# A retention layer and a gated feed-forward block on one core: the steps of a hand-written order split by engine and put in a new order

## The chip, the cores and the metric

The kernel runs on one core of a Trainium2 chip. A core has five engines that run their own instruction lists and wait for each other through semaphores: PE (matrix products, with weight loads, PEld, beside them), DVE (vector), ACT (scalar functions and copies), POOL (GpSimd, which here also issues the loads), and SP (which issues the stores and the DMA transposes). The metric is the device time of one execution in microseconds. The profile is of one execution.

## The reference

```python
def _attn_ref(q, k, v):                       # 4 x 8 x 768 x 64
    gamma = 1.0 - 2.0 ** (-5.0 - np.arange(H, dtype=np.float32))
    scale = 1.0 / np.sqrt(D)
    ...
    for t in range(S):
        state = gamma[None, :, None, None] * state + np.einsum('bhd,bhe->bhde', k[:, :, t], v[:, :, t])
        y[:, :, t] = scale * np.einsum('bhd,bhde->bhe', q[:, :, t], state)
...
def _moe_ref(x, w_gate, w_val, w_out):        # 3072 x 512, 512 x 1536, 1536 x 512
    gate = 1.0 / (1.0 + np.exp(-(x @ w_gate)))
    val = x @ w_val
    return (gate * val @ w_out).astype(np.float32)
```

The attention's output, with the heads side by side as 512 features of 3072 tokens, is the input x of the feed-forward part. Inputs and outputs are float32.

## The kernel before

**Tiling.** The sequence is cut into 6 chunks of 128 positions. A chunk of all four batches is one stage t: 512 tokens. Its attention is done in two halves, P = 2t and 2t + 1, of two batches each; c is the batch in a half. So P runs from 0 to 11 and t from 0 to 5.

**Attention of a half P.** `load` brings k, q and v to SBUF as bf16 (three DMAs on POOL's queue). The transposes of k and q, `qkT`, come from PE (`transposes`, evicted by ACT) for the first halves and from DMA transposes on SP's queue (`xbar`) for P from 4 on. `scores` (16 matmuls for each c, into two PSUM banks) give q times k; `masks` (DVE, line 208) multiply them by the decay table `maskd` and free the banks; `inter` and `intra` (lines 217, 223) add the part of the carried state and of the chunk itself; `y_out` (DVE, line 238) writes the result into `xT`, the transposed input of the feed-forward part. `scaled` (ACT, line 194, or DVE, line 190) weights k, `state` (PE) multiplies it with v, `state_sum` (DVE) adds to the running state `za`, and `state_out` (ACT, line 260) copies it to `zbd`. `tile_tables` (POOL, lines 151 and 155) builds the decay tables of a stage.

**Feed-forward of a stage t.** There are 12 groups of 128 hidden features. A gate product goes through a sigmoid (ACT) and is multiplied with a value product (DVE or POOL) into `hT`. Stages 0 and 2 and the last two groups of stages 3 to 5 use `up`, whole products; stage 1 works in halves of 256 tokens (`up_half`); stages 3 to 5 make the value products of two groups at a time with seven half-size products (`val_product`, a fast matrix multiplication), which need sums of the weights (`val_weight_sums`, POOL, `ws`) and of x (`x_sums`, DVE, `xs`), with ACT copies and DVE additions between the products (lines 395 to 407). The second matrix product of a stage, `product` with `fast_out`, is done in the same way with seven products for each of two token blocks i; it needs `hidden_sums` (DVE, line 438, `hs`) and `weight_sums` (POOL and ACT, `wt`). For block 1 of stage 0 it is done plainly (`down`), and the hidden sums of stage 0 (`s`) are of 128 columns instead of 256. Between product 5, 6, 7 and 4 of a block lie an ACT copy (lines 480 to 494, tile `p`) and a DVE addition (lines 481 to 490, tile `ob`) that read the bank onto which the next product adds. In stages 1 to 4 `mm` splits each matmul of 128 columns in two of 64.

**Order.** The kernel is scheduled by hand: each engine runs its instructions in the order in which the program issues them. After a fixed beginning (first loads, tables, the attention of P = 0 and 1, the first group of stage 0, and the loads up to P = 5) the strings in ORDER, one for each stage, list steps. A step is a letter and a number; `-` puts it in the stage before, `@` names a stage. A step issues all that belongs to it on all engines: `u3` is a gate product, a value product, the sigmoid and the multiply of group 3; `B5` is the scores, inter, intra, state products, masks, y_out and state sum of a half; `X5` is product 5 of block 0 with its copy and addition. `H` (`hold`) and `I` keep POOL waiting until the DMA transposes of a half, or a stage's hidden sums, are there, before the next loads or weight sums.

**Room.** PSUM has 7 banks for all of this (`bank`, pool `pf`) and one for the states; a product's step begins when one of the seven is free. There are 4 buffers each of k, q, v and qkT, two of kt, six for sigmoids (`gs`), two for `scr`, four for `ob`.

Of the kernel before, what the change touches and what calls it, by code (L numbers as in the profile page):

```python
# [17 lines left out]
def kernel(  # L18
# [10 lines left out]
    nc = tc.nc  # L29
# [118 lines left out]
    def tile_tables(t):  # L148
        maskd[t] = at.tile([128, 2, NP, C], F32, tag="maskd", name="maskd")
        for i in range(2):  # L150
            nc.gpsimd.affine_select(maskd[t][:, i], tabk[:, t, i:H:2].unsqueeze(2).to_broadcast([128, NP, C]),
                                    pattern=[[0, NP], [1, C]], base=0, channel_multiplier=-1,
                                    compare_op=ALU.is_ge, fill=0.0)
        taby[t] = at.tile([128, NP, C], F32, tag="taby", name="taby")
        nc.gpsimd.tensor_tensor(taby[t], taby0, tabz[:, t, :].unsqueeze(2).to_broadcast([128, NP, C]), op=ALU.mult)
# [11 lines left out]
    def transposes(P, i, cs, *evict):  # L167
        tp = bank([128, 2 * NP, C], BF16).rearrange("d (c p) s -> d c p s", c=2)
        x = (kn, qn)[i][P].rearrange("s g d -> s (g d)")
        for c in cs:  # L170
            for p in range(NP):
                nc.tensor.transpose(tp[:, c, p, :], x[:, (c * NP + p) * C:(c * NP + p + 1) * C], ident)  # L172
        if len(evict) == 1:
            cs = [slice(cs[0], cs[-1] + 1)]
# [3 lines left out]
    def xbar(P):  # L178
        new_qkT(P)
        for i, x in enumerate((kn, qn)):  # L180
            nc.sync.dma_start_transpose(out=qkT[P][:, i].rearrange("d c p s -> d (c p) s"),
                                        in_=x[P].rearrange("s g d -> s (g d)"))

    def scaled(P, part, eng=None):
        x = kn[P].rearrange("s (c h) d -> s c h d", c=2)
        if part in (None, 0):
            kt[P] = ld.tile([C, 2 * H, D], BF16, tag="kt", name="kt", bufs=2)
        to = kt[P].rearrange("s (c h) d -> s c h d", c=2)
        if part is None:
            eng.tensor_tensor(to, x, tabk[:, P // 2, :].unsqueeze(1).unsqueeze(3).to_broadcast([C, 2, H, D]),  # L190
                              op=ALU.mult)
            return
        for h in range(part * NP, (part + 1) * NP):
# [9 lines left out]

    def masks(P, c):
        st[P, c] = []
        for i in range(2):
            s = at.tile([128, NP, C], BF16, tag="st", name="st", bufs=8)
            nc.vector.tensor_tensor(s, sc[P, c][i], (mask0 if P < 2 else maskd[P // 2])[:, i], op=ALU.mult)  # L208
            st[P, c].append(s)
# [10 lines left out]
    def intra(P, c):  # L220
        for p in range(NP):
            for i in range(2):
                nc.tensor.matmul(y[P, c][i * D:(i + 1) * D, p, :], heads(vn[P], c)[:, 2 * p + i, :],  # L223
                                 st[P, c][i][:, p, :], start=(P < 2 and p == 0), stop=True, skip_group_check=True)
# [31 lines left out]
    def state_out(P):  # L256
        j = P % 2
        for i in range(2):
            half = slice(i * D, (i + 1) * D)
            nc.scalar.copy(zbd[j][half, :, :, half], za[j][half])  # L260

    def has_state(P):
        return P is not None and P < NPAIR - 2

    def block(done, new, sum_now=True):
        if new is not None:
            for c in range(2):
                scores(new, c)
        if done is not None:
            for c in range(2):  # L270
                inter(done, c)
            for c in range(2):
                intra(done, c)
        if has_state(new):
            state(new)
        if new is not None:
            for c in range(2):
                masks(new, c)
        if done is not None:
            for c in range(2):  # L280
                y_out(done, c)
        if has_state(new) and sum_now:
            state_sum(new)
# [15 lines left out]
    def up(t, n1, lo=0, hi=512, finish=True):  # L299
        if t not in hT:  # L300
            hT[t] = ffn.tile([128, NFF, 512], BF16, tag="hT", name="hT", bufs=2)
        ps = []
        for w in (wg, wv):
            u = bank([128, 512])
            for kk in range(KT):
                mm(t, u[:, lo:hi], w[:, kk, n1 * 128:(n1 + 1) * 128], xT[t][:, kk, lo:hi],
                   start=(kk == 0), stop=(kk == KT - 1))
            ps.append(u)
        gs = ffn.tile([128, 512], F32, tag="gs", name="gs", bufs=6)
        gated[t, n1] = (hT[t][:, n1, lo:hi], gs[:, lo:hi], ps[1][:, lo:hi], ps[0][:, lo:hi])  # L310
        if finish != "none":
            up_sigmoid(t, n1)
        if finish is True:
            up_finish(t, n1)

    def up_sigmoid(t, n1):
        nc.scalar.activation(gated[t, n1][1], gated[t, n1][3], AX.Sigmoid)  # L317

    def up_finish(t, n1):
        to, gs, val, _ = gated.pop((t, n1))  # L320
        nc.vector.tensor_tensor(to, gs, val, op=ALU.mult)  # L321

    def up_half(t, n1, half):
        lo = half * 256
        if t not in hT:
            hT[t] = ffn.tile([128, NFF, 512], BF16, tag="hT", name="hT", bufs=2)
        ps = []
        for w in (wg, wv):
            u = bank([128, 2, 256])
            for i in range(2):  # L330
                for kk in range(KT):
                    mm(t, u[:, i], w[:, kk, (n1 + i) * 128:(n1 + i + 1) * 128], xT[t][:, kk, lo:lo + 256],
                       start=(kk == 0), stop=(kk == KT - 1))
            ps.append(u)
        gs = ffn.tile([128, 2, 256], F32, tag="gs", name="gs", bufs=6)
        nc.scalar.activation(gs, ps[0], AX.Sigmoid)
        nc.vector.tensor_tensor(hT[t][:, n1:n1 + 2, lo:lo + 256], gs, ps[1], op=ALU.mult)
# [3 lines left out]
    def val_weight_sums(g, eng):  # L341
        lo, hi = (slice(n * 128, (n + 1) * 128) for n in (2 * g, 2 * g + 1))
        a11, a12, a21, a22 = wv[:, :2, lo], wv[:, 2:, lo], wv[:, :2, hi], wv[:, 2:, hi]
        s1, s2, s3, s4 = (ws[:, g, i] for i in range(4))
        eng.tensor_tensor(s1, a21, a22, op=ALU.add)
        eng.tensor_tensor(s2, s1, a11, op=ALU.subtract)
        eng.tensor_tensor(s3, a11, a21, op=ALU.subtract)
        eng.tensor_tensor(s4, a12, s2, op=ALU.subtract)
# [3 lines left out]
    def x_sums(t):  # L352
        xs[t] = ffn.tile([128, 4, KT // 2, 256], BF16, tag="xs", name="xs", bufs=1)
        b11, b12, b21, b22 = (xT[t][:, kk:kk + 2, c:c + 256] for kk in (0, 2) for c in (0, 256))
        t1, t2, t3, t4 = (xs[t][:, i] for i in range(4))
        nc.vector.tensor_tensor(t1, b12, b11, op=ALU.subtract)
        nc.vector.tensor_tensor(t3, b22, b12, op=ALU.subtract)
        nc.vector.tensor_tensor(t2, b22, t1, op=ALU.subtract)
        nc.vector.tensor_tensor(t4, b21, t2, op=ALU.subtract)

    sig, vals = {}, {}

    def gate(t, n1):
        if t not in hT:
            hT[t] = ffn.tile([128, NFF, 512], BF16, tag="hT", name="hT", bufs=2)
        u = bank([128, 512])
        for kk in range(KT):
            mm(t, u, wg[:, kk, n1 * 128:(n1 + 1) * 128], xT[t][:, kk, :], start=(kk == 0), stop=(kk == KT - 1))
        sig[n1] = ffn.tile([128, 512], F32, tag="gs", name="gs", bufs=6)
        nc.scalar.activation(sig[n1], u, AX.Sigmoid)  # L370

    def val_product(t, g, n):
        lo, hi = (slice(i * 128, (i + 1) * 128) for i in (2 * g, 2 * g + 1))
        if n == 1:
# [301 lines left out]
```

## Time and profile before

| What | Value |
|---|---|
| median of 3 runs | 222.43 us (221.85 to 222.57) |
| profiled execution, first to last instruction | 221.5 us |
| PE busy | 209.5 us, 95% |
| PEld busy | 161.7 us, 73% |
| DVE busy | 158.4 us, 72% |
| POOL busy | 123.7 us, 56% |
| ACT busy | 116.8 us, 53% |
| second half of the first feed-forward group begins on PE | 17.65 us |
| software DMA queue (loads), share of 16 engines | 82.4% |
| hardware DMA queue (stores and transposes) | 27.5% |
| granted TensorE clock | 1.00 |

Busy shares are of the span of 221.5 us. A wait in the lists is the idle time of an engine ahead of an instruction, with what ended it. In the chain each row has a start, a length and what ran. DMA shares of the two queues are of the time that packets took and may add to more than one.

### The profile page before, as it was taken

The numbers are of one execution on the slowest core, as the hardware profiler recorded it, in microseconds if no ns is written. First come the engines' busy times: TensorE is split into PE (matmuls) and PEld (weight loads), VectorE is DVE, ScalarE is ACT, GpSimd is POOL, SyncE is SP. The second block draws the span as 40 slices with busy tenths as digits, with TensorE's granted clock in tenths as the row PEclk, the third lists the DMA queues.
The fourth block names the chain that finished last, engine by engine and source line by source line (L and its number), as shares of the span: only waits on it lengthen the run. The fifth ranks groups of instructions, "written<-read, shape, count | busy, mean of one in ns | idle before, by whom it ended". The sixth has DMA issues, their size and how long they took to land.

```text
span 221.5 us, 6886 instructions
## 1 busy us (share of the span) xinstructions
PE 209.5 (95%) x2924; PEld 161.7 (73%) x2924; DVE 158.4 (72%) x326; ACT 116.8 (53%) x250; POOL 123.7 (56%) x141
## 2 busy tenths in 40 slices
PE   6558999999998999999999999999999999999993
PEld 6444445799997777767779877789877777866682
DVE  6764876988659596465997579898577797544861
ACT  7584375437794336445397277635345525465231
POOL 8966886769997606999400896540243331325500
PEclk9999999999999999999999999999999999999999
DMA  9999999999995999719999899930310000220014
GB/s 126 134 172 194 196 173 156 195 186 157 132 119 53 139 198 140 215 47 120 126 134 199 136 186 157 124 73 0 145 52 0 3 3 0 95 98 0 1 44 150
DMA packets 103999, 25.35 MB, mean 114 GB/s; under 512 B 93984, under 2 KB 101152, under 8 KB 103968
## 3 DMA queue, kind: packets, MB, share of 16 engines
q0 software_dynamic: 81248, 13.90, 82.4%
q1 hardware_dynamic: 22576, 10.88, 27.5%
q8 instruction: 23, 0.38, 0.7%
q10 hardware_dynamic: 144, 0.13, 0.2%
q14 instruction: 8, 0.07, 0.2%
HBM read 28.31 MB, written 6.29 MB: 156 GB/s over the span
## 4 chain that ended last, share of the span: by engine, by line
PE 86%; DVE 5%; DMA 4%; POOL 3%; issue 0%; ACT 0%; POOLq 0%; DVEq 0%
PE ff L297 52%; PE ff L293 25%; DMA vn<-in_v_dram 4%; PE ff L201 2%; PE ff L217 2%; PE ff L223 2%; DVE xT L238 2%; PE z L245 1%; DVE hs L438 1%; DVE st L208 1%; POOL vn L64 1%; POOL kn L64 1%; POOL qn L64 1%; POOL kn L72 0%; PE ff L172 0%
## 5 line engine op out<-in xcount | busy, mean ns | idle before, releaser
L297 PE MATMUL ff<-xT,wg 128*64 128x512 bf16 (+1 forms) x480 | 50.3, 337 | 0.3 <-DVE xT L238 0.2
L401 POOL TENSOR_TENSOR hT<-gs,scr 128x512 bf16<-128x512 f32 x15 | 19.4, 1293 | 35.4 <-DVE scr L400 35.4
L297 PE MATMUL ff<-xT,wv 128*64 128x256 bf16 (+1 forms) x400 | 35.6, 307 | 1.0 <-DVE st L208 1.0
L297 PEld LDWEIGHTS <-wg 128*64 128x64 bf16 x480 | 27.7, 110 | 7.3 <-issue 0.3
L297 PEld LDWEIGHTS <-wv 128*64 128x64 bf16 x440 | 26.2, 110 | 8.8 <-issue 1.2
L321 DVE TENSOR_TENSOR hT<-gs,ff 128x512 bf16<-128x512 f32 (+1 forms) x31 | 20.6, 666 | 15.0 <-ACT gs L317 6.0
L370 ACT ACTIVATE gs<-ff 128x512 f32<-128x512 f32 x30 | 17.9, 597 | 22.3 <-PE ff L297 12.9
L317 ACT ACTIVATE gs<-ff 128x512 f32<-128x512 f32 (+1 forms) x31 | 17.8, 582 | 20.6 <-PE ff L297 11.5
L293 PE MATMUL ff<-xT,wg 128*128 128x512 bf16 (+1 forms) x100 | 25.0, 371 | 1.5 <-ACT xT L236 0.9
L208 DVE TENSOR_TENSOR st<-ff,maskd 128x512 bf16<-128x512 f32 x40 | 24.8, 682 | 1.5 <-PE ff L201 1.5
L297 PEld LDWEIGHTS <-hT 128*64 128x64 bf16 x384 | 21.4, 110 | 3.8
L405 POOL TENSOR_TENSOR hT<-gs,scr 128x256 bf16<-128x256 f32 x15 | 11.3, 756 | 12.5 <-DVE scr L404 12.5
L293 PE MATMUL ff<-xT,wv 128*128 128x512 bf16 (+1 forms) x80 | 17.5, 342 | 0.0
L260 ACT CAST zbd<-za 64x512 bf16<-64x512 f32 x20 | 12.3, 616 | 8.8 <-DVE za L252 3.2
L297 PE MATMUL ff<-wo,hT 128*64 128x256 bf16 (+1 forms) x216 | 16.2, 296 | 0.0
L293 PEld LDWEIGHTS <-wg 128*128 128x128 bf16 x100 | 9.4, 98 | 9.2 <-issue 0.9
L64 POOL DMA_DIRECT2D vn<-in_v_dram x12 | 14.0, 1170 | 2.9 <-PE ff L297 1.7
L194 ACT ACTIVATE kt<-kn,tabk 128x128 bf16<-128x128 bf16 x48 | 15.2, 390 | 0.1
L64 POOL DMA_DIRECT2D kn<-in_k_dram x11 | 12.9, 1173 | 3.2 <-DMA vn<-in_v_dram 1.5
L297 PEld LDWEIGHTS <-hs 128*64 128x64 bf16 x252 | 14.0, 110 | 0.9
L293 PEld LDWEIGHTS <-wv 128*128 128x128 bf16 x90 | 8.8, 98 | 7.6 <-issue 0.2
L64 POOL DMA_DIRECT2D qn<-in_q_dram x11 | 12.7, 1158 | 1.3 <-issue 0.6
(108 smaller groups left out, 412.3 us busy)
## 6 DMA issues: line engine op xcount, KB each, us to landing
out_dram<-ob SPq DMA_DIRECT2D x22, 256.0 KB, 2.6
vn<-in_v_dram POOLq DMA_DIRECT2D x12, 256.0 KB, 12.1
kn<-in_k_dram POOLq DMA_DIRECT2D x11, 256.0 KB, 8.5
qn<-in_q_dram POOLq DMA_DIRECT2D x11, 256.0 KB, 11.8
wo<-in_moe_w_out_dram POOLq DMA_DIRECT2D x4, 384.0 KB, 13.0
wg<-in_moe_w_gate_dram POOLq DMA_DIRECT2D x5, 256.0 KB, 9.8
wv<-in_moe_w_val_dram POOLq DMA_DIRECT2D x5, 256.0 KB, 9.5
out_dram<-ob SPq DMA_DIRECT2D x3, 128.0 KB, 2.2
```

Source lines behind the costliest of these rows:

```text
L64: nc.gpsimd.dma_start(out=held[P], in_=src(x, P))
L194: nc.scalar.activation(to[:, :, h, :], x[:, :, h, :], AX.Copy, scale=tabk[:, P // 2, h:h + 1])
L201: nc.tensor.matmul(sc[P, c][i][:, p, :], qkT[P][half, 0, c, p, :], qkT[P][half, 1, c, p, :], start=True, stop=True)
L208: nc.vector.tensor_tensor(s, sc[P, c][i], (mask0 if P < 2 else maskd[P // 2])[:, i], op=ALU.mult)
L260: nc.scalar.copy(zbd[j][half, :, :, half], za[j][half])
L293: nc.tensor.matmul(o, left, right, skip_group_check=True, **kw)
L297: nc.tensor.matmul(o[half], left[:, half], right, skip_group_check=True, **kw)
L317: nc.scalar.activation(gated[t, n1][1], gated[t, n1][3], AX.Sigmoid)
L321: nc.vector.tensor_tensor(to, gs, val, op=ALU.mult)
L370: nc.scalar.activation(sig[n1], u, AX.Sigmoid)
L401: nc.gpsimd.tensor_tensor(hT[t][:, 2 * g], sig[2 * g], v[:, 0:2].rearrange("p two n -> p (two n)"), op=ALU.mult)
L405: nc.gpsimd.tensor_tensor(hT[t][:, 2 * g + 1, 256:], sig[2 * g + 1][:, 256:], v[:, 2], op=ALU.mult)
```

## The change

Each function that issued work on several engines is split, so that a step issues one operation, or the matmuls of one product. A step's name has two letters now, and `+` and `-` after its number move it a stage later or earlier (twice for two). The 1016 steps of ORDER are all written in a new order. The fixed beginning has the same instructions in the same order. No instruction is added or removed; the compiled lists have the same numbers of each operation on each engine, with 2924 matmuls, and the same DMAs on each queue (54 on POOL's, 43 on SP's, one on ACT's). The core of the diff:

```diff
-    def tile_tables(t):
-        maskd[t] = at.tile([128, 2, NP, C], F32, tag="maskd", name="maskd")
-        for i in range(2):
+    def tile_tables(t, i):
+        if i < 2:
+            if t not in maskd:
+                maskd[t] = at.tile([128, 2, NP, C], F32, tag="maskd", name="maskd")
...
+    def mask(P, c, i):
+        st[P, c, i] = at.tile([128, NP, C], BF16, tag="st", name="st", bufs=8)
+        nc.vector.tensor_tensor(st[P, c, i], sc[P, c][i], (mask0 if P < 2 else maskd[P // 2])[:, i], op=ALU.mult)
...
-    def up(t, n1, lo=0, hi=512, finish=True):
...
+    def up(t, n1, which, lo=0, hi=512):
+        if (t, n1, which) not in us:
+            us[t, n1, which] = bank([128, 512])
+        w = (wg, wv)[which]
+        for kk in range(KT):
+            mm(t, us[t, n1, which][:, lo:hi], w[:, kk, n1 * 128:(n1 + 1) * 128], xT[t][:, kk, lo:hi],
+               start=(kk == 0), stop=(kk == KT - 1))
...
-    def hidden_sums(t, g, n=256, parts=range(4)):
+    def hidden_sums(t, g, i, n=256, eng=nc.vector):
...
-        for i in parts:
-            o, x, z, op = ops[i]
-            nc.vector.tensor_tensor(o, x, z, op=op)
+        eng.tensor_tensor(o, x, z, op=op)
...
-    def fast_out(t, i, n):
+    def fast_copy(t, i, n):
...
+    def fast_add(t, i, n):
...
+    def fast_store(t, i, n):
...
     STEPS = {
-        "u": lambda t, n: up(t, n),
-        "a": lambda t, n: up_half(t, n, 0),
-        "S": lambda t, g: hidden_sums(t, g),
-        "s": lambda t, g: hidden_sums(t, g, 128),
-        "X": lambda t, n: products(t, (0, n)),
-        "B": lambda t, P: block(P - 1, P if P < NPAIR else None),
...
+        "gm": lambda t, n: up(t, n, 0),
+        "vm": lambda t, n: up(t, n, 1),
+        "sg": lambda t, n: up_sigmoid(t, n),
+        "mu": lambda t, n: up_finish(t, n),
+        "ag": lambda t, n: up_half(t, n, 0, 0),
+        "av": lambda t, n: up_half(t, n, 0, 1),
+        "as": lambda t, n: half_sigmoid(t, n, 0),
+        "am": lambda t, n: half_finish(t, n, 0),
...
+        "vp": lambda t, n: half_product(t, n // 10, n % 10, 1),
+        "vc": lambda t, n: val_copy(t, n // 10, n % 10),
+        "va": lambda t, n: val_add(t, n // 10, n % 10),
+        "vf": lambda t, n: val_finish(t, n // 10, n % 10),
+        "aw": lambda t, n: halves_sums(wv, n // 4, ws[:, n // 4], n % 4),
+        "xs": lambda t, n: x_sums(t, n),
+        "hs": lambda t, n: hidden_sums(t, n // 4, n % 4),
+        "hh": lambda t, n: hidden_sums(t, n // 4, n % 4, 128),
+        "wp": lambda t, n: weight_sums(n // 4, n % 4),
+        "dp": lambda t, n: product(t, n // 10, n % 10),
+        "dc": lambda t, n: fast_copy(t, n // 10, n % 10),
+        "da": lambda t, n: fast_add(t, n // 10, n % 10),
+        "ds": lambda t, n: fast_store(t, n // 10, n % 10),
+        "dm": lambda t, n: down(t, n // 2, n % 2),
...
+        "lk": lambda t, P: load(P, "k"),
+        "ho": lambda t, P: hold(P),
+        "xk": lambda t, P: xbar(P, 0),
+        "xq": lambda t, P: xbar(P, 1),
+        "tp": lambda t, n: transpose(n // 2, n % 2, [0, 1]),
+        "kt": lambda t, n: scaled(n // 8, n % 8),
+        "sc": lambda t, n: scores(n // 2, n % 2),
+        "in": lambda t, n: inter(n // 2, n % 2),
+        "ia": lambda t, n: intra(n // 2, n % 2),
+        "sm": lambda t, P: state(P),
+        "mk": lambda t, n: mask(n // 4, n // 2 % 2, n % 2),
+        "yo": lambda t, n: y_out(n // 2, n % 2),
...
     ORDER = [
-        "u1 u2 k0 u3 k1 u4 Z0 u5 u6 Z1 s0 u7 u8 J4 J5 k2 u9 T2 u10 f2 p11",
...
+        "gm1 tt7+ kt0 gm2 vm1 sm0 gm3 gm5 vm5 wp0+ sg1 kt8 sg5 vm3 wp1+ aw10++ gm6 gm4 sg3 zs0 sg2 mu3 sg6 wp2+  "
+        "sg4 vm2 gm9 gm8 mu5 mu1 vm4 zo0 vm6 gm10 mu4 sg8 gm7 sg9 wp8+ sg7 sg10 tp4 mu2 xk4 kt16 vm9 vm8 hh0 mu6  "
+        "mu8 tp5 vm10 zo1 te4 wp3+ vm7 te5 sc5 sc4 gm11 mu10 vm11 mk10 mk11 in5+ mk8 mk9 in4+ ia5+ ia4+ xq4 yo5+  "
+        "yo4+ sm1 zs1 tp7+ wp4+ tp6+ sg11",
+        "ag6 wp5 sm2- mu9- mu7- te7 te6 as6 av0 sc6 mu11- sc7 ag10 kt24 mk13 xk5- ag4 zo3- mk15 zo2- tt11 ag0  "
...
+        "bv10 aw2+ bv6 bs10 bm4 ho5 bs2 lk6 bs0 kt39 bs8 hh2- dc05- wc4 wp11 kt33 kt44 kt35 hh10- bm2 da05-  "
+        "dp03- kt47 kt45 sc9 bm6 mk19 bm10 sc8 bv8 bv0 kt42 wc5 dc06- mk18 dp06- dm2- kt43 lq6 sc11 tt8 mk17 lv6  "
...
+        "mk20 mk22 in10 da07- hs8 dp04- mk21 tt16++ kt40 hs9 kt46 yo9 in11 ia8 hs4 ia11 aw4+ aw5+ ia10 hs0 dc04-  "
+        "kt41 dp02 aw0+ ds06- dm6- yo11 kt53+ dp11 xk6 hs10 yo10 dp01 xq6 dp15 yo8",
...
+        "gm1 gm0 kt48 dt1-- gm3 kt54 sg3 hs11- sg1 kt51 xk7- hs5- kt59 sm5- aw18 dp05- zs4- dm7-- kt55 gm4 zo8-  "
+        "sg0 dc15- aw1 hs2- xq7- hs1- dc05- hs3- kt56 gm7 vm3 do3-- aw6 dp16- tt14 vm7 kt60 kt52 aw8 vm2 sg7  "
+        "hi0- da05- aw7 mu3 hs7- gm2 hs6- gm5 ho7 dp13- dp03- vm0 sg2 lk8 kt63 mu7 dp06- mu2 dp12- dc06- mu0  "
+        "da06- dp07- sg5 sc13 da15- da07- ds04-- sc12 vm1 aw9 sg4 dc16- dp04- mk27 dt3-- lq8 mk25 kt49 zo9- gm6  "
...
+        "vp11 dp05- yo18- xs0 vp1 hs6- dc05- hs5- dp02- dp12- xs2 vp15 zo17- dp06- hs7- dc15- vc15 vp2 vp5 da05-  "
+        "vp16 vc5 hs11- xs3 xs1 dp03- da15- zo19- vp3 dc06- gm1 da06- va5 vp6 sg1 hs2- hs10- dp13- gm0 vp13 vc16  "
+        "dc16- dp07- xq11- dp16- da07- da16- va16 dp04- dp17- sc21 vc6 va6 da17- sc20 vp7 dp14- zo18- gm2 ds06-  "
...
     for t, order in enumerate(ORDER):
         for s in order.split():
-            at_t = t
-            if s[0] == "-":
-                s, at_t = s[1:], t - 1
...
-            STEPS[s[0]](at_t, int(s[1:]))
+            at_t = t + s.count("+") - s.count("-")
+            s = s.strip("+-")
+            STEPS[s[:2]](at_t, int(s[2:]))
```

Steps that begin with `gp`, `gc`, `ga`, `gs`, `dw` and `hg` exist in the changed STEPS but stand nowhere in ORDER.

More of the change, by code (lines that the diff above doesn't have):

```diff
@@ L254, in state_sum, with state_out @@
             nc.vector.tensor_tensor(za[j], za[j], zz[P], op=ALU.add)
[L256 to L283, printed above, removed]
+    def state_out(P, i):
+        half = slice(i * D, (i + 1) * D)
+        nc.scalar.copy(zbd[P % 2][half, :, :, half], za[P % 2][half])
     hT = {}
@@ L313, in up, with half_sigmoid @@
[L313 to L323, printed above, removed]
-        lo = half * 256
[L325 to L337, printed above, removed]
+    def half_sigmoid(t, n1, half):
+        gated[t, n1, half] = ffn.tile([128, 2, 256], F32, tag="gs", name="gs", bufs=6)
+        nc.scalar.activation(gated[t, n1, half], us[t, n1, half, 0], AX.Sigmoid)
@@ L361 @@
[L361 to L372, printed above, removed]
[L373 to L377 removed]
+        t1, t2, t3, t4 = (xs[t][:, j] for j in range(4))
```

341 lines of the change are left out of this document (191 added, 150 removed), and 49 rows, old and new, of the table ORDER.

## The prediction

> **What bounds the kernel now.** I read the page's first part, then the busy time by stretch, the list of what PE waited for after 18 us, and the chain of waits around the one long wait.
>
> ```profile
> span 221.5 us, 6886 instructions
> ...
> PE 209.5 (95%) x2924; PEld 161.7 (73%) x2924; DVE 158.4 (72%) x326; ACT 116.8 (53%) x250; POOL 123.7 (56%) x141
> ```
> ```profile
> 0.00:10.00 10.00, 5.93 (x69) 5.23 (x70) 6.46 (x23) 6.43 (x23) 9.10 (x15) 1.00 1.42 127
> 10.00:20.00 10.00, 6.86 (x93) 4.88 (x94) 6.21 (x12) 6.23 (x12) 7.09 (x11) 1.00 1.92 177
> ...
> 60.00:70.00 10.00, 9.00 (x180) 8.46 (x176) 6.74 (x12) 7.69 (x21) 8.27 (x10) 1.00 0.97 85
> ...
> 210.00:222.00 12.00, 7.99 (x73) 6.74 (x70) 4.83 (x13) 2.78 (x8) 0.00 (x0) 0.97 0.25 89
> ```
> ```profile
> PE ff L297 <- DVE st L208: 1.0, 1, 1.0
> PE ff L297 <- DVE xT L238: 0.2, 1, 0.2
> ```
> The columns of the second fence are PE, PEld, DVE, ACT and POOL busy, the granted clock, DMA share and GB/s. PE misses 4.1 and 3.1 us in the first two stretches, 1.0 in 60 to 70, and 4.0 at the end; elsewhere it is full, at a granted clock of 1.00. The start (to 17.65 us, where the second half of `up(0, 0)` begins) is written above ORDER and is not changed. The end (last matmul, one ScalarE copy, last store, closing) has the same last steps in both lists. So what an order can move is PE's lost time between 17.65 and 218 us, and the third fence shows how little that is: 1.2 us. The place of the large one:
>
> ```profile
> 65.58 0.55 PE ff L201 x16
> 66.13 0.37 PE z L245 x16
> 66.50 0.89 PE ff L297 x16
> 67.40 0.04 issue
> 67.44 0.06 DVE hs L438
> 67.49 0.15 issue
> 67.64 0.69 DVE st L208
> 68.33 0.04 issue
> 68.38 6.28 PE ff L297 x88
> ```
> Sixteen gate matmuls end their issue at 67.4, and the value ones start at 68.38: the PSUM bank they need is freed by a mask (L208), and that mask stands on DVE behind four hidden sums (L438). Timed by starts (66.33 plus 16 matmuls at 0.054 us is 67.20) PE is 1.18 late. The chain of the whole run gives PE to DVE at three more places: at 42.94 and 82.01 (a gate step waits for `y_out`'s xT) and at 208.99 (a product of the last value group waits for an addition). The wait at 82.01 is 0.2; I take 0.2 for the other two as well. Lost by order now: 1.18 + 3 x 0.2 = 1.8 us.
>
> **The change, part by part.** Nothing is added or removed: PE has 2924 weight loads and 2924 matmuls in both, DVE, ACT and POOL have the same operations, and the DMAs are the same. Inside a step (a gate step's four matmuls, a product's six or twelve) nothing moves. PE pays for the array's shape when it changes: state matmuls are due at 24.70 + 0.86 = 25.56 and start at 25.66, so 0.10 each; the old order has 38 such changes, the new 37. That is nothing in the sum. PE's work being equal, the sum is made of waits.
>
> *Waits that go.* (a) The 1.18 at 68.38: in the new list the sums of 128 columns (`hh`) stand one by one between half-step multiplies, none directly ahead of the masks of P = 4 (`sc9 bm6 mk19 bm10 sc8 bv8 bv0`), and gate and value steps are apart, so a late bank is asked for later. Gain 1.18; lower bound 0, if another DVE queue takes its place. (b) 42.94: `yo5 yo4` are followed on PE by `sm1 tp7 tp6` (0.37 + 0.89) before `ag6`, where the old order has the two transposes alone (0.89); 0.37 more cover against 0.2. (c) 82.01: after the last `ia10` PE has `dp02 dm6 dp11 dp01 dp15`, four products at 0.65 and one down half at 1.30, 3.9 us, while DVE still has two sums and three `yo` (2 x 0.42 + 3 x 0.60 = 2.6). Gone. (d) 208.99: the groups of stage 5 are interleaved, other products lie between; gone. Together 1.18 + 0.6 = 1.8.
>
> *Waits that come.* They are found by laying the new PE list beside the DVE and ACT lists, with these rows:
>
> ```profile
> L485 ACT COPY p<-ff x11: 372/372/374, 72.7 to 214.6; 128x256 f32<-128x256 f32 x11
> L487 DVE TENSOR_TENSOR ob<-p,ff x11: 420/420/422, 73.1 to 215.4; 128x256 f32<-128x256 f32 x11
> ...
> DMA to landing us min/median/max: 11.0/11.7/12.5
> ```
> (the first two from the view of tile p, the last from that of kn between 20 and 37 us). (e) Stage 0: the new list asks for weights and for kn of P = 2 earlier. From 18.66 there are 16 steps of 0.86 (`gm1 ... gm7`) and the state step with its change of shape (0.47) ahead of `tp4`: 18.66 + 13.76 + 0.47 = 32.9. That kn was issued at 22.54 and lands 11.0 later, at 33.5. PE waits 0.6, or less if the weight slices on the way hold it first (`vm5` needs a slice that lands at about 23.6, just when PE gets there); between 0.3 and 0.9, I take 0.5. The old order needed it at 35.16. (f) Stage 2, `dp06- dp12- dc06- mu0 da06- dp07-`: dp07 adds onto the bank that dc06 copies and da06 reads. From the end of dp06's issue: 0.17 for its results, copy 0.37, addition 0.42, three hand-overs of about 0.05: 1.1 us. Under it lies only dp12, 0.65. Wait 0.45; idle engines cannot shorten a chain that begins with dp06 itself, so at least 0.4, and 0.9 with one more copy or addition ahead in a queue. The old order had `X6 u3 X7`, 1.73 of cover. (g) Stage 4, `dc16- dp07- xq11- dp16-`: dp16 waits for dc16, which stands on ACT behind vc16, which waits for `vp13`, the PE step just ahead of dp07: 0.17 for its results, two copies (0.27 and 0.37), two hand-overs, 0.9; cover dp07, 0.65. From 0 to 0.5, I take 0.25. Together 1.2.
>
> Sum: -1.8 + 1.2 = **-0.6 us**.
>
> *Queues beside them.* On SP, the transposes `xk5 xq5` are now apart and `xq5` stands behind more steps, yet waits for qn of P = 5 as before. POOL's hold shows that the last of them had landed by 68.15. Counting the new list to `sc11` (24 half steps at 0.87, five products, one down half at 1.30, scores, inter, intra and state) PE gets there at about 71, against 74.65: 2.9 us of cover are left of 6.5. POOL has the weight sums (`wp`, `aw`) spread over stages 0 to 3, and loads of P = 6 and 7 behind them, up to 3 us later than at 68.61; their first use is at about 96, their landing under 90. Hidden. Stores cost nothing until the end, where the order is the same.
>
> The profiled span of 221.5 stands 0.9 below the 222.43 median of the runs, which the profile has no lines for; I keep it. 221.5 - 0.6 = 220.9 of span, **221.8 us** as measured.
>
> **The rivals.**
>
> *Slower: hidden sums held by POOL.* The rows of L438:
> ```profile
> L438 DVE TENSOR_TENSOR hs<-hT 128x256 bf16<-128x256 bf16 x3 | 3.0, 1000 | 0.0
> L438 DVE TENSOR_TENSOR hs<-hs,hT 128x256 bf16<-128x256 bf16 x3 | 2.4, 810 | 0.1
> L438 DVE TENSOR_TENSOR hT<-hT 128x256 bf16<-128x256 bf16 x3 | 1.8, 600 | 0.0
> L438 DVE TENSOR_TENSOR hs<-hT,hs 128x256 bf16<-128x256 bf16 x3 | 0.8, 280 | 0.0
> ```
> Undisturbed such a sum takes 0.28; the first at 65.81 took 1.19, ending just after POOL's multiply of L155. A sum that starts while POOL works waits for POOL's instruction to end. In the old order the sums come in fours, so the first waits and the rest get through; in the new one eleven stand singly in stage 1, where POOL is busy 4.84 of every 5 us (50 to 65). If all are held by 0.72, DVE gets 7.9 us more there instead of 4.7. DVE is idle 0.9 to 3.2 us in each of these stretches, which covers most; where a bank or an xT is behind one, PE pays up to 0.9 (1.19 - 0.29). Two such places cost 1.8, and 222.43 - 0.6 + 1.8 = 223.6. It decides from 1.3 us of uncovered holding on. For it: the wait at 68.38 had just this cause. Against it: splitting also puts multiplies and masks between the sums. The Trainium skill, page "SBUF — State Buffer", section "SBUF: two separate sides", says that VectorE and GpSimd share a port pair as an exclusive lock: whoever starts first keeps it for the whole instruction and the other is blocked. The long sums here agree (1.19 against 0.28). By that rule alone, with every single sum meeting a POOL instruction and nothing covering, the order would be slower, as in this rival.
>
> *No net change.* (a) is replaced by a wait of like size, since all seven banks stay in use: 1.18 of returned wait at most; half of it, 0.6, takes the gain back: 222.4. For it: the chains through ACT and DVE run close behind PE (DVE's additions into scr wait for ACT's copies 11 times, 7.4 us in all), so a small shift can open a new wait. Against it: the new list has no place of that size that I could find.
>
> *A larger gain.* (e), (f) and (g) come out at their lower ends, 0.3 + 0.4 + 0 = 0.7: 222.43 - 1.8 + 0.7 = 221.3; if waits too short for the list (under 0.1 each) go as well, an estimate of 0.4 more, 220.9. For it: gate and value steps apart give many banks a later date. Against it: three waits would all have to be at their best. With PE's work the same, the floor for any order is 222.43 - 1.8 - 0.4 = 220.2.
>
> **How the numbers follow.** Forecast (a small gain, 221.4 to 222.2) 0.45; no net change 0.20; a larger gain 0.17; slower 0.18. A measurement of this kernel tells 0.3% (0.67 us) from no change, so "faster" begins at 221.76, within the forecast's own range: a little over half of it (0.25) and all of the third rival make 0.42, the rest and the second rival 0.40, slower 0.18. The range goes from 220.9, the lower end of the larger gain, to 223.4, which leaves out about half of the slower rival.
>
> **What would show it.** Right: PE's list of waits after 18 us without a mask at 68; a wait for kn at about 33; one of 0.4 to 0.5 on a product of stage 2 for an addition into ob; the last matmul at about 217.4 instead of 218.0. Wrong: PE waits over 0.5 in stage 1 behind L458 sums of over 1 us; a score waiting for a DMA transpose near 71; more than 2.4 us of PE waits after 18 us; or another mean duration of PE's groups, which would mean that equal instructions do not make equal work.

## The result and the profile after

The changed kernel takes 230.66 us (median of 4 runs, 228.92 to 231.16) against 222.5 us of the kernel before on the same chip (221.85 to 222.76): a ratio of 1.036, 95% interval 1.031 to 1.040. It is slower by 8.2 us. The profiled execution took 230.31 us, with a span of 228.4 us; the one shown before had 221.5. A few executions fell into a slower state (one took 560 us where its fellows took 225 to 228), and the medians here leave them out.

The engines' row of the page of the kernel after:

```profile
span 228.4 us, 6858 instructions
...
PE 211.3 (93%) x2917; PEld 161.2 (71%) x2924; DVE 162.4 (71%) x326; ACT 113.1 (50%) x250; POOL 125.3 (55%) x141
```

The span grew by 6.9 us and PE's busy time by 1.8 of them (7 matmul records are missing); so most of it, 5.1 us, is time in which PE stood still. Its waits after 18 us (us in total, times, longest), and two stretches of the span (columns as before):

```profile
PE ff L286 <- DVE xT L252: 3.8, 1, 3.8
PE ff L176 <- DMA kn<-in_k_dram: 0.9, 1, 0.9
PE ff L286 <- DVE ob L512: 0.3, 1, 0.3
```
```profile
50.00:60.00 10.00, 6.22 (x126) 6.05 (x122) 10.00 (x7) 1.66 (x4) 7.39 (x8) 0.97 2.13 158
60.00:70.00 10.00, 10.00 (x174) 10.00 (x172) 7.16 (x16) 6.29 (x13) 4.09 (x5) 0.86 0.82 76
```

The wait for the mask is gone. The waits for kn and for ob are the ones that the forecast expected, at their places. New is one of 3.8 us between 54.4 and 58.2, while DVE is "busy" for the whole ten microseconds with seven instructions. After it the granted clock is 0.86 on average. Cut finer, that loss of clock is one stretch right behind the wait (the same columns):

```profile
59.30:62.70 3.40, 3.40 (x50) 3.40 (x47) 3.40 (x8) 1.62 (x3) 0.00 (x0) 0.51 1.59 138
62.90:66.00 3.10, 3.10 (x62) 3.10 (x59) 2.25 (x8) 1.93 (x4) 0.09 (x1) 1.00 1.14 118
```

PE is full for 3.40 us and does 50 matmuls at a clock of 0.51, and 62 in the 3.10 us after. DVE in the stretch from 49 us, and then POOL, both from the timeline (start, length, engine, line):

```profile
49.01 0.69 DVE L326 TENSOR_TENSOR hT<-gs,ff 128x512 bf16<-128x512 f32 x1 [0.35 <-ACT gs L322]
49.61 0.68 DVE L458 TENSOR_TENSOR hs<-hT 128x256 bf16<-128x256 bf16 x1
50.22 7.32 DVE L458 TENSOR_TENSOR hs<-hs,hT 128x256 bf16<-128x256 bf16 x1
57.46 1.27 DVE L252 TENSOR_TENSOR xT<-ff,taby 128x512 bf16<-128x512 f32 x2
```
```profile
50.10 0.73 POOL L337 TENSOR_TENSOR ws<-wv 128x256 bf16<-128x256 bf16 x1
50.79 1.14 POOL L441 TENSOR_TENSOR scr<-scr,wo 128x512 f32<-128x512 f32 x1
51.90 1.15 POOL L441 TENSOR_TENSOR wt<-wo 128x512 bf16<-128x512 bf16 x1
53.01 1.16 POOL L441 TENSOR_TENSOR wt<-wo,scr 128x512 bf16<-128x512 bf16 x1
54.14 1.14 POOL L441 TENSOR_TENSOR wt<-wo 128x512 bf16<-128x512 bf16 x1
55.25 1.14 POOL L441 TENSOR_TENSOR scr<-wo 128x512 f32<-128x512 bf16 x1
56.36 1.03 POOL L157 TENSOR_TENSOR taby<-taby,tabz 128x512 f32<-128x512 f32 x1
```

One hidden sum, 0.28 us of work, is on record for 7.32. It begins 0.12 us after POOL begins the first of these seven instructions, which follow each other without a gap (each starts 0.03 to 0.05 us before the one ahead ends), and it ends 0.15 us after the last. Behind it in DVE's list stand the two `y_out` that write xT, and the gate half step on PE waits for these. In the kernel before POOL's list has small gaps, and no sum there is held over more than one or two instructions. POOL and DVE there:

```profile
53.98 1.04 POOL L155 TENSOR_TENSOR taby<-taby,tabz 128x512 f32<-128x512 f32 x1
54.98 1.20 POOL L417 TENSOR_TENSOR wt<-wo 128x512 bf16<-128x512 bf16 x1
56.15 1.20 POOL L418 TENSOR_TENSOR scr<-wo 128x512 f32<-128x512 bf16 x1
57.42 1.29 POOL L419 TENSOR_TENSOR scr<-scr,wo 128x512 f32<-128x512 f32 x1
```
```profile
54.40 0.77 DVE L438 TENSOR_TENSOR hs<-hT 128x256 bf16<-128x256 bf16 x1
55.20 1.13 DVE L438 TENSOR_TENSOR hs<-hs,hT 128x256 bf16<-128x256 bf16 x1
56.26 1.24 DVE L438 TENSOR_TENSOR hT<-hT 128x256 bf16<-128x256 bf16 x1
```

L419 reads what L418 wrote and starts 0.07 us after its end (57.35 to 57.42): the third sum ends just behind this gap, at 57.50. The first two got in without one: they end at 55.17 and 56.33, 0.2 us after POOL began L417 and L418, each of which starts a little before the instruction ahead has ended. The new order puts other sums between the dependent ones (`wp1 aw10 wp2 wp8 wp3`), and the gaps are gone.

A second change is at the very end. The last store goes out from ACT's queue in both kernels; start and length of its issue, before and after:

```profile
218.43 0.37 ACTq L496 DMA_DIRECT2D out_dram<-ob  x1
```
```profile
223.28 2.54 ACTq L524 DMA_DIRECT2D out_dram<-ob  x1
```

The issue takes 2.54 us instead of 0.37, and SP, which waits for the last stores to land, gets them 1.9 us later after its own last issue (a wait of 3.8 us against 1.9). In the DMA view of 223.2 to 224.4 us stands a transfer of instructions, two packets (the kernel before has one, between 217.9 and 218.4 us, ahead of its store):

```profile
q14 instruction: 2, 0.02, 6.4%
```

### The profile page after: what moved, and what is told of

Its sections match the earlier page's. It is cut to its first block, busy times and chain, and to the rows that moved or that the text cites. A ratio compares the mean times of both kernels' runs of the same rounds, so it can differ in the third digit from the quotient of the medians.

```text
span 228.4 us, 6858 instructions
## 1 busy us (share of the span) xinstructions
PE 211.3 (93%) x2917; PEld 161.2 (71%) x2924; DVE 162.4 (71%) x326; ACT 113.1 (50%) x250; POOL 125.3 (55%) x141
## 4 chain that ended last, share of the span: by engine, by line
PE 78%; DMA 12%; DVE 4%; POOL 2%; issue 1%; ACT 1%; POOLq 0%; ACTq 0%
PE ff L286 51%; PE ff L282 19%; DMA kn<-in_k_dram 5%; DMA wg<-in_moe_w_gate_dram 4%; DVE hs L458 3%; DMA vn<-in_v_dram 3%; PE ff L214 2%; PE ff L231 2%; PE ff L237 2%; PE z L259 1%; PE ff L176 1%; POOL kn L64 1%; POOL qn L64 0%; POOL kn L72 0%; POOL qn L72 0%
## 5 line engine op out<-in xcount | busy, mean ns | idle before, releaser
L306 ACT ACTIVATE gs<-ff 128x512 f32<-128x512 f32 (+1 forms) x61 | 35.3, 590 | 39.2 <-PE ff L286 22.8
L286 PE MATMUL ff<-xT,wg 128*64 128x512 bf16 (+1 forms) x480 | 48.1, 340 | 3.8 <-DVE xT L252 3.8
L286 PE MATMUL ff<-xT,wv 128*64 128x256 bf16 (+1 forms) x400 | 36.2, 313 | 0.0
L286 PEld LDWEIGHTS <-wv 128*64 128x64 bf16 x440 | 24.4, 112 | 6.5
L219 DVE TENSOR_TENSOR st<-ff,maskd 128x512 bf16<-128x512 f32 x40 | 25.8, 682 | 3.4 <-PE ff L214 3.4
L397 DVE TENSOR_TENSOR scr<-scr,ff 128x256 f32<-128x256 f32 x45 | 17.9, 416 | 10.8 <-PE ff L282 4.8
L282 PE MATMUL ff<-xT,wg 128*128 128x512 bf16 (+1 forms) x94 | 23.5, 370 | 1.8 <-ACT xT L250 0.9
L512 DVE TENSOR_TENSOR ob<-p,ff 128x256 f32<-128x256 f32 x33 | 13.5, 416 | 15.4 <-ACT p L500 5.4
L207 ACT ACTIVATE kt<-kn,tabk 128x128 bf16<-128x128 bf16 x48 | 17.1, 399 | 0.6 <-DMA kn<-in_k_dram 0.6
L458 DVE TENSOR_TENSOR hs<-hs,hT 128x512 bf16<-128x512 bf16 (+1 forms) x18 | 16.6, 924 | 0.1
```

Of the source, the lines that this page charges most:

```text
L207: nc.scalar.activation(to[:, :, h, :], x[:, :, h, :], AX.Copy, scale=tabk[:, P // 2, h:h + 1])
L219: nc.vector.tensor_tensor(st[P, c, i], sc[P, c][i], (mask0 if P < 2 else maskd[P // 2])[:, i], op=ALU.mult)
L282: nc.tensor.matmul(o, left, right, skip_group_check=True, **kw)
L286: nc.tensor.matmul(o[half], left[:, half], right, skip_group_check=True, **kw)
L306: nc.scalar.activation(gated[t, n1][:, lo:hi], us[t, n1, 0][:, lo:hi], AX.Sigmoid)
L397: nc.vector.tensor_tensor(o, o, (b if n == 5 else ac)[:, :256], op=ALU.add)
```

## The experiments

Unless said otherwise an edit is made to the kernel after, and times are medians beside runs of the kernel before on the same chip (222.4 to 222.9 us in the four sessions).

**The held sum elsewhere.** The second sum moves out of POOL's long run:

```diff
-        ... wp9 hh1-  yo7 yo6 ag8 ...  am4 am8 am10 hh5- hh7- ...
+        ... wp9  yo7 yo6 ag8 ...  am4 am8 am10 hh5- hh1- hh7- ...
```

> One hidden sum of stage 0 (the second on DVE in stage 1, held for 7.3 us at 50.2) is moved down DVE's list behind four multiplies and the first sum of its group; PE, ACT and POOL keep their lists. Theory 'held sum' (POOL's unbroken run of seven instructions keeps the sum, and with it the xT writes behind it, and PE idles 3.8 us and then runs 3.4 us at half the clock): no DVE instruction over 3.5 us, PE's wait for xT gone, 221.0 to 223.0 us. Rival 'tight everywhere' (the new order has little slack and this wait only stands for the others): other waits come in its place, 226 or more.

225.99 us, ratio 1.017 (1.012 to 1.022): 4.7 us of the 8.2 are back, and no DVE instruction is over 3.5 us, as the theory expected; the time lies 3.0 us above its band and at the edge of the rival's. xT is written at 53.55, while POOL works without a gap, and the two `y_out` take the normal 1.29 us together; so it is not DVE as a whole that waits for POOL, but the hidden sums. The next sum, `hh4` at 55.95, was held for 2.40 us, to the end of the same run of POOL, and PE lost 0.9 us behind it.

**Gaps given back to POOL.** Dependent value sums stand next to each other again, DVE's list is untouched:

```diff
-        ... vm3 wp1+ aw10++ ... sg6 wp2+ ... te4 wp3+ vm7 ...
+        ... vm3 wp1+ wp2+ wp3+ aw10++ ... sg6 ... te4 vm7 ...
```

> DVE's list is that of the changed kernel; on POOL the four weight sums of the first group stand together again, so that the third and the fourth wait for the one ahead and POOL pauses for 0.08 us each time. Theory 'held sum': the sum gets in at such a pause, held under 2 us, 221.0 to 223.5 us. Rival 'its neighbour' (the sum is held because it follows another sum on DVE without a wait between them, whatever POOL does): held 5 us or more as before, 228 to 231. Rival 'tight everywhere': 226 or more with the sum short.

225.46 us, ratio 1.012 (1.009 to 1.016). The same two sums take 0.58 and 0.28 us, and PE's wait for xT is gone, though each of the sums stands where it stood. The time is 2.0 us above the band expected. What is left to the kernel before is mostly the tail: the last store's issue still takes 2.44 us.

**The sum's neighbours.** `hh8` moves ahead of the multiply, so that the two sums are no longer side by side:

```diff
-        ... wp6 am0 tt9 hh8- wc0 ... wp9 hh1-
+        ... wp6 hh8- am0 tt9 wc0 ... wp9 hh1-
```

> POOL's list is that of the changed kernel; on DVE the first sum is moved ahead of the multiply before it, so that a multiply stands between the two sums. Theory 'held sum': the second sum still meets POOL's unbroken run and is held to its end near 57.4, 5 us or more, 228 to 231 us. Rival 'its neighbour': it gets in at the next change of instruction on POOL, held under 1.5 us, 221 to 223.5.

225.41 us, ratio 1.017 (1.010 to 1.024). The second sum started at 49.60, under the instruction ahead of L337, and was through after 0.64; this is what the rival expected of it, and not the theory, which had it held for 5 us or more. But `hh4` at 54.95, which stands behind a multiply, was then held for 2.54 us, to the end of POOL's run at 57.34. So a sum is caught without another sum ahead of it: standing side by side is not the cause. The sums arrive some tenths of a microsecond earlier or later than in the kernel after; that this decides which one is caught is not shown.

**The kernel before without gaps.** In the old order six value-weight sums are put between the dependent ones (the same instructions, which stood later in POOL's list):

```diff
-        "W": lambda t, g: weight_sums(g, nc.gpsimd),
+        "W": lambda t, g: weight_sums(g, nc.gpsimd, ((g, 0), (g, 2))),
```

> The kernel before, with six of POOL's later value weight sums moved up between the weight sums of stage 1, so that no weight sum there stands directly behind the one it needs and POOL's pauses of 0.08 us are filled. Theory 'held sum': at least one hidden sum of stage 1 near 54 to 66 is held over more than two POOL instructions (2.5 us or more), PE waits behind it, 224 to 231 us. Rival 'its neighbour' or 'tight everywhere': sums are held over one instruction each as before, 222 to 223 us.

234.08 us, ratio 1.052 (1.048 to 1.056): the old order becomes slower than the new one. DVE's timeline and two stretches:

```profile
57.15 13.28 DVE L453 TENSOR_TENSOR hs<-hT 128x256 bf16<-128x256 bf16 x1
70.46 0.29 DVE L453 TENSOR_TENSOR hs<-hs,hT 128x256 bf16<-128x256 bf16 x1
```
```profile
60.00:70.00 10.00, 3.42 (x64) 3.25 (x59) 10.00 (x1) 5.58 (x14) 10.00 (x12) 0.81 0.71 79
70.00:80.00 10.00, 8.19 (x124) 7.89 (x125) 6.33 (x15) 2.36 (x6) 7.34 (x8) 0.68 1.66 107
```

One sum was held for 13.28 us, over some fifteen POOL instructions, and PE waited 8.4. The band expected was 224 to 231. The cause can be put into the old order, and it acts there in the same way.

**One gap, in the middle of the run.** `wp2` stands behind `wp8`, so that one dependent pair is left, as third and fourth of the run:

```diff
-        ... mu3 sg6 wp2+ ... sg9 wp8+ sg7 ...
+        ... mu3 sg6 ... sg9 wp8+ wp2+ sg7 ...
```

> The kernel after with one change: the weight sum wp2 stands behind wp8, so that in the run of POOL that held the hidden sum for 7.3 us (50.2 to 57.4) the dependent pair wp2 wp3 comes third and fourth, with a pause of 0.08 us between them at about 53.1; the other boundaries stay as they are. Theory 'held sum, let in at the first pause': the sum that starts at 50.2 takes 2.8-3.0 us and ends at about 53.2, the wait of PE for xT falls from 3.8 to under 0.3 us, no window at half clock at 59-63; the slow last store stays, so 225.0-226.2 us. Rival 'held until POOL has nothing to do': the sum takes 7 us or more and the time stays at 230-231. Rival 'it is the sum's own operands': 7.3 us as well.

225.17 us, ratio 1.013 (1.007 to 1.019). DVE and POOL:

```profile
48.98 3.61 DVE L458 TENSOR_TENSOR hs<-hT 128x256 bf16<-128x256 bf16 x1
52.52 0.28 DVE L458 TENSOR_TENSOR hs<-hs,hT 128x256 bf16<-128x256 bf16 x1
```
```profile
50.19 1.15 POOL L441 TENSOR_TENSOR wt<-wo 128x512 bf16<-128x512 bf16 x1
51.30 1.14 POOL L441 TENSOR_TENSOR scr<-scr,wo 128x512 f32<-128x512 f32 x1
52.52 1.30 POOL L441 TENSOR_TENSOR wt<-wo,scr 128x512 bf16<-128x512 bf16 x1
```

A gap from 52.44 to 52.52, 0.08 us, ended the hold. Here it was the first sum that was caught, 1.2 us earlier, so its hold is longer than expected and ends as expected, at the gap; POOL worked on for 4.5 us more, to 57.10.

**The last store from SP**, on the kernel with the gaps given back:

```diff
-            (nc.scalar if i else nc.sync).dma_start(out=out[rows[1], :256], in_=hi[:, :256])
+            nc.sync.dma_start(out=out[rows[1], :256], in_=hi[:, :256])
```

> The kernel after with the three value weight sums standing one behind the other (as in the run with pauses, 225.46 us, whose last ACT store took 2.44 us to issue), and the last store sent from SP's queue instead of ACT's. Theory 'instruction fetch': the store itself is quick; ACT's list reaches the end of a block of instructions there and waits for the next one. From SP the issue takes 0.4 us or less, the stretch from PE's last matmul to the end falls from about 5 us to 3.2-3.7, and the time to 223.2-224.0 us. Rival 'the store's own data path' (this row of the output waits or is written slowly whoever sends it): the issue or the landing stays about 2 us longer and the time stays at 225.2-225.7.

224.29 us, ratio 1.007 (1.004 to 1.009), 1.2 us less than with ACT's store and 0.3 over the band expected. The two last stores now go out one behind the other, 0.82 us for both. So the store itself is not slow.

**Ten more instructions on ACT**, on the same kernel, the store left on ACT:

```diff
     keep_on(30)
+    for _ in range(10):
+        nc.scalar.copy(kept[:, 4:5], ident[:, :1])
     tables()
```

> The kernel of the run with pauses, last store on ACT as in the kernel after, with ten copies of one column put into ACT's list before the first list of steps, where ACT has room; so ACT's list is as long as in the kernel before (326 instructions there, 336 here and before). Theory 'instruction fetch': the block boundary no longer falls on the store, whose issue takes 0.37 us again as in the kernel before; time 223.2-224.0 us. Rival 'the order of the end' (the store is slow because of what stands ahead of it at the end, which is unchanged): issue 2.2-2.5 us, time 225.2-225.8.

223.44 us, ratio 1.004 (1.000 to 1.008), in spite of ten instructions more. The store's issue:

```profile
218.39 0.37 ACTq L524 DMA_DIRECT2D out_dram<-ob  x1
```

ACT's list had become ten entries shorter (324 for 334 in the traces: 70 waits are written as entries of their own, where the kernel before has 80; the operations are the same). With the old length the same store, behind the same work, takes 0.37 us again. In the traces in which ACT sends it, it takes 0.37 us wherever it is the 330th entry on record (the kernel before, the one without gaps, and the three with ten more) and 2.14 to 2.54 us wherever it is the 320th (the kernel after and six others). So it is the store's place in the list that made it slow, and the end's order is not to blame.

**PE kept at work in the wait, twice.** 32 matmuls of 256 columns, in one kernel ahead of step `bg10` (group 10, second half), in another ahead of `ag8` (group 8, first half); the diff is that of the first:

```diff
         us[t, n1, half, which] = u = bank([128, 2, 256])
+        for _ in range(32 if (t, n1, half, which) == (1, 10, 1, 0) else 0):
+            nc.tensor.matmul(u[:, 0], ident, wg[:, 0, :256], start=True, stop=True)
```

> The kernel after, with 32 matmuls of 256 columns put ahead of the half step that waits for xT (stage 1, step bg10), into the bank that this step clears anyway: PE works 3.5 of the 3.8 us that it stood idle, and the held sum stays as it is. Theory 'the idle time costs clock': the window at half clock (59.3 to 62.8 in the profile of the kernel after) is gone, mean granted clock 0.998 or more, and the time is 228.8-229.3 us, 1.3 to 1.8 below the 230.66 of the kernel after. Rival 'the clock falls for another reason' (the load of the stage): a window of half clock stands there all the same, and the time is 230.3-231.2. Rival 'the filling costs more than it saves': over 231.5, with PE's wait for xT gone and its next steps later by more than 4.2 us.

> As the run with 32 more matmuls of 256 columns, which measured 234.37 us because they stood behind the step that waits and so only came on top (3.7 us of wait, then 4.3 us of added work at half clock). Here the same 32 stand ahead of the first half step that waits for xT (stage 1, step ag8), so PE works in the 3.7 us that it stood idle. Theory 'the idle time costs clock': no window of half clock follows at 59-63, the mean granted clock is 0.992 or more in nearly all runs (a window at the very start counts 0.008 and costs little), and the time is 228.7-229.4 us, 1.3 to 1.9 below the 230.66 of the kernel after. Rival 'the clock falls for another reason': a window of half clock in the profile all the same between 57 and 66, and a median of 230.3-231.2.

234.37 and 233.74 us: the added work came on top both times. In the first, `ag8`, ahead of the added matmuls, was the step that waited. In the second the added matmuls waited themselves: the bank that they clear is the one that the late `y_out` reads. PE in the second:

```profile
57.65 3.65 PE L315 MATMUL ff<-wg,ident 128*128 128x256 bf16 x32 [4.01 <-DVE xT L252]
61.24 1.94 PE L286 MATMUL ff<-xT,wg 128*64 128x256 bf16 x32
```

So the hole could not be filled in this way. But the runs of the second kernel answer part of the question. Its profiled execution had the wait of 4.01 us and no stretch at half clock behind it: mean granted clock 0.993, 231.35 us. Four other runs had mean clocks of 0.974 to 0.986 and took 233.3 to 234.8 us. The kernel after shows the same: one run at 0.999 took 228.92 us, the three at 0.974 to 0.981 took 230.3 to 231.2. A lower clock goes with 1.4 to 3.4 us; that the idle time causes it was not tested by an edit. In two other profiles the clock fell while PE still stood idle: at 66.17 us in the kernel before without gaps (idle from 63.42 to 71.81), and at 58.87 in the one with matmuls ahead of `bg10` (idle from 55.38 to 59.07).

**The two small waits taken out**, on the kernel with the gaps and ten ACT instructions (the ten copies stand later here, behind the loads for P = 2 and 3):

```diff
-        ... sg10 tp4 mu2 xk4 kt16 vm9 vm8 hh0 ...   da06- dp07- sg5 sc13 da15- ...
+        ... sg10 mu2 xk4 kt16 vm9 tp4 vm8 hh0 ...   da06- sg5 sc13 dp07- da15- ...
```

> The kernel with the ten more copies on ACT (223.44 us: the value weight sums in sequence, the last store quick again), with the two waits that the new order brought to PE taken out: the transposition tp4 stands behind vm9, 1 us of matmuls later, and the product dp07 of stage 2 behind sg5 and sc13. Theory of the account (held sums, slow last store, and two small waits of 0.6 and 0.3 us are all that the new order costs): PE's waits for kn and for ob fall by 0.5-0.8 us in all, and the time is 222.5-223.0 us, within 0.2% of the kernel before (222.4-222.9). Rival 'the gain of the new order shows once its costs are gone': 221.8-222.3, under the kernel before by the 0.4-0.6 us that was forecast. Rival 'each shift only moves the wait to the next instruction': 223.2-223.7, with another wait of the same size beside it.

223.22 us beside 222.87, ratio 1.000 (0.997 to 1.003). The waits for kn and ob are gone; 0.3 us for qn come, and 0.6 near 62 us stay, for which the trace names nothing that PE waited for. The time is in the band of the last rival, that each shift only moves the wait.

**That stop near 61 us**, with a gate half step put ahead of the product that stopped:

```diff
-        ... hh5- hh7- dp01- wc2 dp05- bs6 hh9- bg0 bs4 ...
+        ... hh5- hh7- wc2 bg0 dp01- dp05- bs6 hh9- bs4 ...
```

> The last kernel (223.22 us, level with the kernel before) with one more move: the gate half step bg0 (0.87 us of matmuls) stands ahead of the product dp01 of stage 0 at about 61 us, whose second group of matmuls waited 0.6-0.8 us with nothing named as the releaser, while the hidden sum that it reads was held by two instructions of POOL in turn. Theory 'an uncovered hold of one POOL instruction, as the forecast priced it': the 0.6 us go, the time falls by 0.3-0.6 to 222.6-222.9 us, ratio to the kernel before 0.995-0.999. Rival 'the time at 61 us is PE's own (fetching its instructions)': a stop of 0.5-0.8 us near 61-63 stays, wherever dp01 stands, and the time stays at 223.0-223.4.

222.76 us beside 222.45, ratio 0.999 (0.996 to 1.002). The time fell into the theory's band, but by luck, for the stop stayed, behind the first matmul of the half step that now stands there, which does not read a hidden sum:

```profile
60.77 0.27 PE L286 MATMUL ff<-xT,wg 128*64 128x256 bf16 x1
61.59 1.03 PE L286 MATMUL ff<-xT,wg 128*64 128x256 bf16 x15 [0.55 <-issue]
```

So the held sum was not its cause. In six of the edited kernels PE stops at this place, the 736th matmul of its list. No transfer of instructions is in the DMA view between 61 and 62.5 us either; what stops PE there stays open.

## Why the prediction was wrong

**The step that failed** is the price of one held sum in the slower rival: "A sum that starts while POOL works waits for POOL's instruction to end", and "PE pays up to 0.9 (1.19 - 0.29)". In the forecast's own sum the holding stood at nothing, since DVE's idle time and the multiplies between the sums were to cover it. The mechanism was named, and at the right stretch (50 to 65 us); its size was not. A sum that does not get in at a change of instruction can wait until POOL's run pauses or ends: 0.58 us with a gap near, 3.61 with a gap after four instructions, 7.32 over seven, 13.28 over some fifteen. One instruction is the price only where the sum gets in at the first change. The forecast's total was almost right: it put 7.9 us of holding on DVE in stage 1, and the twelve sums of 128x256 took 11.8 us for 3.4 of work (12 x 0.28), 8.4 of holding. But 7.0 of it fell on one sum, past every cover, where the forecast spread it over eleven with 0.7 each. The trace of before shows only a part of this: of the three long sums at 54 to 57.5 us one got in at a gap and two at the first change of instruction, and none is held longer, so the price of a longer hold could not be read there. That the gaps go could be read from the new POOL list.

The Trainium skill, page "SBUF — State Buffer", section "SBUF: two separate sides", has the port pair that VectorE and GpSimd share taken for one whole instruction by whoever starts first. Here the sum was passed over at the start of one POOL instruction after another, six in the kernel after (50.79 to 56.36). There the measurement goes beyond that page and decides: POOL without a pause can keep VectorE's sum out for its whole run, not for one instruction.

**Two terms were missing from the sum.** First, the clock after a long wait of PE. In the profile of the kernel after, PE works 3.40 us at a granted clock of 0.51 behind its wait of 3.8; at full clock that work is 1.73, so up to 1.7 us are lost there. The Trainium skill, page "TensorE: Matmul & The Clock Gate", section "Part 1: The HAM clock gate (the "warmup" mystery)", puts TensorE back to half clock after an idle window of about 3.4 us, and has that window run freely. The traces agree with windows that run freely: in the kernel after both stretches at half clock are 3.42 us long (8.14 to 11.56 and 59.34 to 62.76 us), and they begin 51.20 us apart, 15 such lengths. They differ on the idle window: in the length ahead of the second stretch (55.93 to 59.34) PE worked for 1.15 us, and the clock fell all the same. The wait of 4.0 in the run with matmuls ahead of `ag8` fell on two such lengths (counted on from 11.24 us, the first change of its clock on record), with 1.44 and 1.38 us of work in them, and the clock stayed full. So how a wait falls on these lengths may decide; no run tests that. Second, the end: "The end has the same last steps in both lists", and "Stores cost nothing until the end, where the order is the same". The steps are the same, but ACT's list reaches them ten entries earlier, and the last store was 2.54 us in issue: 2.0 us between the two runs (225.46 to 223.44 with ten instructions more).

**The account.** Each is taken against the kernel before of its own session: the kernel after is 8.2 us behind it, the one with the gaps 3.0 (225.46 against 222.44), the one with ten more ACT instructions 0.7 (223.44 against 222.78). So the held sum and the clock are 5.2 us (in the profile 3.8 of waiting and up to 1.7 at half clock, 5.5), and the last store is 2.3. The 0.7 that are left are at the edge of what the interval tells.

**The forecast's own sum** of -0.6. Right: the wait of 1.18 for the mask is gone and its place was not taken by another bank's; the wait for kn came (0.9, forecast 0.5, at its upper bound), the one for an addition into ob too (0.3, forecast 0.45); the one in stage 4 did not come. The mean duration of the large groups is unchanged where the clock is (379 ns for 128x512 gate matmuls and 273 for 128x256, before and with the gaps given back), so equal instructions were equal work. Misread: the 0.2 of the list is the wait at 42.94 (0.16), not the one at 82.01; at 82.01 and 208.99 the list has none, so the 0.2 each there were too much. With 1.2 to 1.4 gone and 1.2 come the sum is about 0, and the kernels with the gaps, the old ACT length and the two waits covered measure 1.000 and 0.999 of the kernel before. A gain of 0.6 us would be 0.997, still inside both intervals; so it was neither shown nor excluded.

**The sign that was named** for being wrong, "PE waits over 0.5 in stage 1 behind L458 sums of over 1 us", is just what the profile shows; so is "more than 2.4 us of PE waits after 18 us" (3.8 + 0.9 + 0.3 = 5.0). The slower case had a chance of 0.18 and a price of 1.8 us; the list of the new order would have allowed a bound: seven POOL instructions with no dependent pair side by side, about 7 us, with two `y_out` behind the sum.

## What to carry to other kernels

When GpSimd's work is put in a new order, look at its gaps as well as at its length: instructions that wait for each other leave short pauses, and a VectorE sum that is kept out by GpSimd gets in at those, if not before; put independent ones between them and one small sum can wait for the whole run, with all that stands behind it. Price a possible hold by the longest unbroken run, not by the longest hold that the old order shows. And compare the ends of two profiles even where the last steps are the same, since the place of an instruction in its engine's list can cost microseconds.

## What the runs showed of the hardware

- Only the hidden sums were held (bf16 in SBUF on both sides, 0.28 us alone). Multiplies and `y_out`, which read PSUM, ran beside POOL at their normal 0.6 to 0.7 us in the same stretch.
- A gap of 0.07 to 0.08 us in POOL's work ended a hold in each of the three kernels looked at (the one before, and those with all gaps and with one). A change of instruction without a gap often did too, as a rule the first that the sum met: at 54.98 and 56.15 in the kernel before, and for the sum at 49.61 in the kernel after when L337 followed L441 at 50.10. One in the kernel with a single gap did not get in at 49.56, at the same change. The sums held for 2.4 us or more, in all these kernels, got in only at a gap or where POOL's run of sums and tables ended. What decides at the first change is open.
- The issue of one store on ACT took 2.1 to 2.5 us in the new order and 0.37 with ten instructions more in the list. The packets of instructions beside it, and the length as the cure, point to ACT waiting for its next instructions; but one such packet also stands beside the quick store of the kernel with ten more, and the trace does not name the wait, so this is an inference.
- In six of the edited kernels PE stopped for 0.3 to 1.3 us, between 61 and 65 us, at the 736th matmul of its list, whatever step stood there, and nothing on record released it.
